# Regrouped weight loads, a first elementwise step by halves, and the last eviction and store on ScalarE, in a dense layer with GELU and its gradients

## The chip, the cores and the metric

The kernel runs on one core of a Trainium2 chip. The metric is the device time of one execution in microseconds. Five engines of the core take part: TensorE (PE in the profile, its weight loads PEld), VectorE (DVE), ScalarE (ACT), GpSimd (POOL) and SyncE (SP), which here only issues DMA transfers. Each engine works through its own instructions in the order in which the program issued them. An instruction that has to wait for another engine or for a transfer holds up all that stands behind it on its own engine.

## The reference

A dense layer with a tanh-approximated GELU is computed, and then the gradients of its five inputs for a given `grad_out`:

```python
B, S, D, F = 1, 2048, 448, 1792        # all bf16
h   = gelu(x @ w1 + b1)                # [S, F]
out = h @ w2 + b2                      # out_0 [S, D]
# gradients of x, w1, b1, w2, b2 for grad_out g [S, D]:
gh  = (g @ w2.T) * gelu'(x @ w1 + b1)  # [S, F]
gx  = gh @ w1.T                        # out_1
gw1 = x.T @ gh ; gb1 = sum(gh, rows)   # out_2, out_3
gw2 = h.T @ g  ; gb2 = sum(g, rows)    # out_4, out_5
```

## The kernel before

The 2048 rows are cut into four blocks b of 512. In each block the 1792 columns of the hidden layer are cut into 14 tiles of 128, taken two at a time, so that a block has seven steps and the whole run has 28, numbered g = 0 to 27. In a step the hidden columns lie on the 128 partitions; its two tiles of 128 columns are the halves h = 0 and 1, each with the 512 rows of the block along a partition, so that an elementwise instruction over a whole step has 1024 elements per partition, and one over a half 512.

The work of one step g, with the names that the text uses:

- `M1(g)` (L213, matmuls L221) and the first half of `rest` (L224, L231) compute u = x w1 in PSUM for both halves: three matmuls of 128 deep and one of 64 each. `rest` (L234) and `M4(g)` (L237, L240) compute q = g w2^T in the same way. There is one buffer for u and one for q. Only for g = 0 does u lie in two tiles of the accumulator pool `acc` instead.
- `act_first` (L243) runs on ACT: V = u + b1 for each half (L247), A = Square of V scaled (L248), hT = GELU of V (L249).
- `dve_first` (L251) runs on DVE: B = (A + const) * V (L252), p = (A + const) * hT (L253), p - 0.5 (L254).
- `act_second` (L256) runs on ACT: t = tanh of B (L257). `dve_second` and `dve_third` (L260, L263) then make t + 1 and the product with p.
- `dve_gate(g)` (L266), called the gate in the text, multiplies with q from PSUM and writes ghT(g).
- `run_pieces` runs the second matmuls (`Unit.piece`, L297). A unit gathers 128 rows of `out` over all 14 tiles of hT, or 128 rows of `gx` over all 14 tiles of ghT, one piece for one tile. In block 0 the four units of `out` grow along with the steps, two pieces each in a step, eight in all; these are called pieces(g). They need hT(g) and rows of w2: pieces(0) need row tiles 0 and 1 of w2, pieces(1) tiles 2 and 3, and so on.

V, A, B have one buffer for all steps, t and p two. The tiles are slices of large flat tensors.

The loop at L359 writes the order out by hand. For step g it issues, on their engines: `rest(g+1, g)`, `M4(g)`, the gate of g, the first ACT and DVE parts of g+1, tanh and the products of g+1, pieces(g), and `M1(g+2)`. At g = 7, `M1(9)` comes ahead of the pieces. Step 0 has no step ahead of it: `M1(0)`, `rest(0)` and its whole elementwise chain stand before the loop (L351 to L358).

All loads of block 0 but those of L168 to L170 are issued on SP in one order (L167, L172 to L175, L186 to L200). Some are plain (`load_w1`: two transfers each, `load_w2`: one), others transposing (`load_x`, `load_g`, `load_w2T`: two each, `load_w1T`: one). `load_w1(f0, f1)` and `load_w2T(f0, f1)` bring the columns f0 to f1 of the hidden layer, of which step g of block 0 uses 256, from 256 g on; `load_w2(t0, t1)` brings row tiles t0 to t1 of w2.

After the 28 steps follow the remaining units, then gw1 (L452, L460), then gw2: 14 tiles of 16 matmuls each (L471), evicted by ACT (L473) and stored by SP. The last of the 14 is evicted by ACT and DVE, half each (L480, L481), and stored by SP (L482).

Of the kernel before, what the change touches and what calls it, by code (L numbers as in the profile page):

```python
# [8 lines left out]
ACT = mybir.ActivationFunctionType  # L9
ALU = mybir.AluOpType  # L10
# [3 lines left out]
GELU_A = 0.044715  # L14
GELU_C = math.sqrt(2.0 / math.pi)
# [3 lines left out]
def kernel(  # L19
# [15 lines left out]
    nc = tc.nc  # L35
    P = 128
    B, S, D = x.shape
# [3 lines left out]
    NF = F // P  # L41
# [8 lines left out]
    NPAIR = NF // 2  # L50
# [8 lines left out]
    out4_v = out_4.rearrange("(ft p) d -> p ft d", p=P)  # L59
# [26 lines left out]
    b1_col = const.tile([P, NF], F32, name="b1_col")  # L86
# [8 lines left out]
    gw2_all = w2_sb  # L95
# [11 lines left out]
    def ring(t, n, g):  # L107
        o = (g % n) * 2 * SB
        return t[:, o:o + 2 * SB].rearrange("p (h s) -> p h s", h=2)

    def hT(g):
        return ring(hT_flat, HR, g)
# [4 lines left out]
    def V_of(g):  # L117
        return VA_flat[:, 0:2 * SB].rearrange("p (h s) -> p h s", h=2)

    def A_of(g):  # L120
        return VA_flat[:, 2 * SB:4 * SB].rearrange("p (h s) -> p h s", h=2)

    def B_of(g):
        return ring(B_flat, 1, g)

    def t_of(g):
        return ring(T_flat, 4, 2 * (g % 2))

    def p_of(g):
        return ring(T_flat, 4, 2 * (g % 2) + 1)  # L130
# [11 lines left out]
    def load_g(b):  # L142
        rows = slice(b * SB, (b + 1) * SB)
        nc.sync.dma_start_transpose(out=gq(b)[:, KF, :], in_=g2[rows, DOV:D])
        nc.sync.dma_start_transpose(out=gq(b)[:, 0:KF, :], in_=g2[rows, 0:DM])  # L145

    def load_w1(eng, f0, f1):
        eng.dma_start(out=w1_sb[:, 0:KF, f0:f1], in_=w1[DL:D, f0:f1].rearrange("(k p) f -> p k f", p=P))
        eng.dma_start(out=w1_sb[0:DL, KF, f0:f1], in_=w1[0:DL, f0:f1])

    def load_w2(eng, t0, t1):
        eng.dma_start(out=w2_sb[:, t0:t1, :], in_=w2[t0 * P:t1 * P, :].rearrange("(t p) d -> p t d", p=P))

    def load_w2T(f0, f1):
        nc.sync.dma_start_transpose(out=w2T_sb[:, KF, f0:f1], in_=w2[f0:f1, DOV:D])  # L155
        nc.sync.dma_start_transpose(out=w2T_sb[:, 0:KF, f0:f1], in_=w2[f0:f1, 0:DM])  # L156
# [14 lines left out]
    nc.scalar.activation(out=T_flat[0:1, SB + 2:SB + 3], in_=ones, func=ACT.Gelu_apprx_tanh)  # L171
    load_g(0)  # L172
    load_w2T(0, 256)
    load_w1(nc.sync, 512, 768)
    load_w2(nc.sync, 0, 2)  # L175
    pw = psum_a.tile([P, SB], F32, name="acc")
    for i in range(8):
        nc.tensor.matmul(pw[:], lhsT=warm[:, 0:P], rhs=warm, start=True, stop=True)
# [4 lines left out]
    nc.vector.tensor_copy(out=b1_col[:], in_=pb[:, 0:NF])  # L183
    for i in range(3):
        nc.tensor.matmul(pw[:], lhsT=warm[:, 0:P], rhs=warm, start=True, stop=True)
    load_w2T(256, 768)  # L186
    load_w2(nc.sync, 2, 6)
    load_w1(nc.sync, 768, 1280)
    load_w2T(768, 1280)
    load_w2(nc.sync, 6, 10)  # L190
    load_w1(nc.sync, 1280, F)
    load_w2T(1280, F)
    load_w2(nc.sync, 10, NF)
    nc.sync.dma_start(out=b2_bc[:], in_=b2.rearrange("(o d) -> o d", o=1).to_broadcast((P, D)))
    load_x(1)
    load_w1T(0, 4)
# [13 lines left out]
    u_of = {}  # L210
# [13 lines left out]
    def rest(gu, gg):  # L224

        if gg is not None:
            q = psum_g.tile([P, 2, SB], F32, name="q")
            g_of[gg] = q
        for h in range(2):
            if gu is not None:  # L230
                nc.tensor.matmul(u_of[gu][h], lhsT=w1_sb[0:DL, KF, cols(gu, h)], rhs=xq(gu // NPAIR)[0:DL, KF, :],  # L231
                                 start=False, stop=True, tile_position=(0, 0), skip_group_check=True)
            if gg is not None:
                nc.tensor.matmul(q[:, h, :], lhsT=w2T_sb[DL:P, KF, cols(gg, h)], rhs=gq(gg // NPAIR)[DL:P, KF, :],  # L234
                                 start=True, stop=False, tile_position=(DL, 0), skip_group_check=True)
# [7 lines left out]
    def act_first(g):  # L243
        u = u_of.pop(g)
        for h in range(2):
            ft = 2 * (g % NPAIR) + h
            nc.scalar.activation(out=V_of(g)[:, h, :], in_=u[h], func=ACT.Identity, bias=b1_col[:, ft:ft + 1])  # L247
        nc.scalar.activation(out=A_of(g), in_=V_of(g), func=ACT.Square, scale=math.sqrt(3.0 * GELU_C * GELU_A))  # L248
        nc.scalar.activation(out=hT(g), in_=V_of(g), func=ACT.Gelu_apprx_tanh)  # L249

    def dve_first(g):  # L251
        nc.vector.scalar_tensor_tensor(out=B_of(g), in0=A_of(g), scalar=3.0 * GELU_C, in1=V_of(g), op0=ALU.add, op1=ALU.mult)  # L252
        nc.vector.scalar_tensor_tensor(out=p_of(g), in0=A_of(g), scalar=GELU_C, in1=hT(g), op0=ALU.add, op1=ALU.mult)  # L253
        nc.vector.tensor_scalar(out=p_of(g), in0=p_of(g), scalar1=-0.5, scalar2=None, op0=ALU.add)  # L254

    def act_second(g):  # L256
        nc.scalar.activation(out=t_of(g), in_=B_of(g), func=ACT.Tanh, scale=-1.0 / 3.0)  # L257

    def dve_second(g):
        nc.vector.tensor_scalar(out=t_of(g), in0=t_of(g), scalar1=1.0, scalar2=None, op0=ALU.add)  # L260
# [89 lines left out]

    M1(0)  # L351
    rest(0, None)
    act_first(0)
    dve_first(0)
    act_second(0)
    dve_second(0)
    dve_third(0)
    M1(1)  # L358
    for g in range(NSTEP):  # L359
# [10 lines left out]
        if nxt is not None:  # L370
            act_first(nxt)
# [71 lines left out]
    for t0, t1 in ((0, 4), (4, HT)):  # L443
        n = (t1 - t0) * P
        for h in range(2):
            a0, a1 = t0 + h * HT, t1 + h * HT
            cs = slice(a0 * P, a1 * P)
            for kt in range(KF):
                ps = psum_a.tile([P, SB], F32, name="acc")
# [6 lines left out]
        ps = psum_a.tile([P, SB], F32, name="acc")  # L456
# [6 lines left out]
        for h in range(2):  # L463
            nc.scalar.dma_start(out=out_2[KF * P:D, (t0 + h * HT) * P:(t1 + h * HT) * P],
                                in_=gw1_rem[h * DL:(h + 1) * DL, t0 * P:t1 * P])


    for ft in range(NF):
        ps = psum_a.tile([P, SB], F32, name="acc")
        for st in range(NS):  # L470
            nc.tensor.matmul(ps[:, 0:D], lhsT=h_blk[ft][:, st, :], rhs=g_all[:, st, :], start=(st == 0), stop=(st == NS - 1))  # L471
        if ft < NF - 1:
            nc.scalar.copy(out=gw2_all[:, ft, :], in_=ps[:, 0:D])  # L473
            if ft % 3 == 2:
                nc.sync.dma_start(out=out4_v[:, ft - 2:ft + 1, :], in_=gw2_all[:, ft - 2:ft + 1, :])
            if ft == NF - 2:
                nc.sync.dma_start(out=out4_v[:, ft:ft + 1, :], in_=gw2_all[:, ft:ft + 1, :])
        else:
            hd = D // 2
            nc.scalar.copy(out=gw2_all[:, ft, 0:hd], in_=ps[:, 0:hd])  # L480
            nc.vector.tensor_copy(out=gw2_all[:, ft, hd:D], in_=ps[:, hd:D])  # L481
            nc.sync.dma_start(out=out4_v[:, ft, :], in_=gw2_all[:, ft, :])  # L482


# [28 lines left out]
```

## Time and profile before

| | |
|---|---|
| median of 3 runs | 278.21 us (277.89 to 278.37) |
| profiled execution, its own time | 278.12 us |
| span of the profile | 276.3 us |
| PE busy in the span | 266.2 us, 96% |
| DVE, ACT, POOL busy | 188.6, 144.5, 50.9 us |
| DVE busy from 7.7 to 14.1 us | 3.83 of 6.40 us |
| DVE busy from 14.1 to 49.8 us | 34.29 of 35.70 us |
| PE busy from 49.8 to 272.7 us | 222.23 of 222.90 us |
| mean granted clock of TensorE | 1.00 |

The page gives the whole span, from the first to the last instruction; the time of an execution has some 1.8 us around it. Instructions that issue transfers are not counted as busy; the profile shows them with a q behind the engine's name (SPq, ACTq). A transfer's landing is counted from the start of its issue. The loads on SP that the change touches, in the order of their issue, as the trace has them:

| load | issued at (us) | issue took (us) | landed after (us) |
|---|---|---|---|
| w2T 0:256, two transposes | 6.66, 7.94 | 1.24, 1.28 | 2.8, 2.9 |
| w1 512:768, two | 9.27, 9.91 | 0.58, 0.56 | 2.8, 2.9 |
| w2 tiles 0:2 | 10.51 | 0.58 | 3.0 |
| w2T 256:768, two | 11.13, 12.34 | 1.16, 1.49 | 3.5, 4.1 |
| w2 tiles 2:6 | 13.87 | 0.58 | 5.78 |
| w1 768:1280, two | 14.51, 15.05 | 0.50, 0.49 | 6.2, 5.9 |
| w2T 768:1280, two | 15.59, 16.90 | 1.27, 3.74 | 5.9, 5.9 |
| w2 tiles 6:10 | 20.69 | 0.59 | 6.0 |
| w1 1280:1792, two | 21.33, 21.87 | 0.50, 0.51 | 6.5, 6.3 |
| w2T 1280:1792, two | 22.42, 25.39 | 2.92, 2.33 | not shown, 4.3 |
| w2 tiles 10:14 | 27.77 | 0.59 | 4.0 |
| b2 | 28.40 | 0.49 | 4.0 |
| x of block 1, two | 28.94, 31.27 | 2.29, 1.26 | 5.1, 3.8 |

### The profile page before, as it was taken

What the parts mean: (1) busy time and instruction counts of PE and PEld (TensorE: products, weight loads), DVE (VectorE), ACT (ScalarE), POOL (GpSimd) and SP (SyncE); (2) the same over time, 40 slices, a digit from 0 to 9 for tenths busy, and PEclk for the clock granted to TensorE, in tenths of its full rate; (3) what the DMA queues carried; (4) which work ended last, traced back from release to release, by engine and by line L of the source; (5) the groups of instructions that cost most, each with busy time, mean ns of one, the idle gap of its engine ahead of it and who ended that gap; (6) DMA issues with size and microseconds to landing.
All of it is one profiled execution on the core that took longest, in us unless ns stands there. A gap on an engine that the chain in (4) does not pass through costs nothing.

```text
span 276.3 us, 3567 instructions
## 1 busy us (share of the span) xinstructions
PE 266.2 (96%) x1389; PEld 123.4 (45%) x1403; DVE 188.6 (68%) x217; ACT 144.5 (52%) x188; POOL 50.9 (18%) x54
## 2 busy tenths in 40 slices
PE   8689999999999999999999999999999999999994
PEld 3234443344344444444444445554444655555552
DVE  0599999999989999999887881109999990000000
ACT  2887888788888878887677750021102121111111
POOL 0000000840120403032030234111510009600000
PEclk9999999999999999999999999999999999999999
DMA  8799999999789955335634329999999971101110
GB/s 168 175 210 209 225 209 186 212 340 154 150 219 188 260 76 120 65 123 118 168 112 78 109 79 214 229 365 208 171 238 250 237 176 57 51 1 50 50 52 33
DMA packets 101571, 43.78 MB, mean 158 GB/s; under 512 B 90161, under 2 KB 98161, under 8 KB 101554
## 3 DMA queue, kind: packets, MB, share of 16 engines
q1 hardware_dynamic: 94224, 26.80, 52.9%
q0 software_dynamic: 4448, 14.69, 17.2%
q10 hardware_dynamic: 2882, 2.07, 2.7%
q8 instruction: 11, 0.18, 0.3%
q14 instruction: 6, 0.05, 0.0%
HBM read 7.00 MB, written 14.23 MB: 77 GB/s over the span
## 4 chain that ended last, share of the span: by engine, by line
PE 82%; DVE 6%; SPq 5%; DMA 2%; ACT 2%; issue 2%; DVEq 0%
PE acc L297 27%; PE acc L471 15%; PE acc L452 13%; PE q L240 11%; PE u L221 9%; PE u L231 4%; PE acc L460 2%; DMA w_gw<-in_w_dram 2%; DVE ghT_h L266 2%; DVE Bt L252 2%; DVE T L253 1%; SPq L156 1%; SPq L155 1%; DVE T L263 1%; SPq L145 1%
## 5 line engine op out<-in xcount | busy, mean ns | idle before, releaser
L297 PE MATMUL acc<-w_gw,hT_h 128*128 128x448 bf16 x224 | 46.1, 352 | 2.4 <-ACT VA L247 1.3
L297 PE MATMUL acc<-w1T_gw,ghT_h 128*128 128x448 bf16 x224 | 45.2, 352 | 0.0
L247 ACT ACTIVATE VA<-u,b_col 128x512 f32<-128x512 f32 x54 | 34.1, 681 | 15.5 <-PE u L231 14.8
L240 PE MATMUL q<-xg_h,w2T_g 128*128 128x512 bf16 x167 | 40.9, 381 | 1.0 <-DMA w2T_g<-in_w_dram 0.8
L266 DVE SCALAR_TENSOR_TENSOR ghT_h<-T,q 128x1024 bf16<-128x1024 bf16 x28 | 34.2, 1220 | 8.8 <-PE q L240 7.6
L221 PE MATMUL u<-xg_h,w_x 128*128 128x512 bf16 x149 | 38.4, 379 | 1.2 <-ACT VA L247 0.6
L252 DVE SCALAR_TENSOR_TENSOR Bt<-VA 128x1024 f32<-128x1024 f32 x28 | 34.1, 1219 | 5.0 <-ACT VA L248 5.0
L452 PE MATMUL acc<-gh_nat,w_x 128*128 128x512 bf16 (+1 forms) x192 | 36.7, 353 | 0.0
L257 ACT ACTIVATE T<-Bt 128x1024 bf16<-128x1024 f32 x28 | 29.6, 1057 | 12.8 <-DVE Bt L252 12.7
L253 DVE SCALAR_TENSOR_TENSOR T<-VA,hT_h 128x1024 bf16<-128x1024 f32 x28 | 34.1, 1219 | 0.0
L297 PEld LDWEIGHTS <-hT_h 128*128 128x128 bf16 x224 | 21.8, 98 | 24.4 <-ACT VA L247 1.8
L297 PEld LDWEIGHTS <-ghT_h 128*128 128x128 bf16 x224 | 21.9, 98 | 20.8
L481 DVE CAST w_gw<-acc 128x224 bf16<-128x224 f32 x1 | 0.4, 391 | 44.5 <-ACT w_gw L480 44.5
L437 DVE TENSOR_TENSOR VA<-VA,gh_nat 128x1792 f32<-128x1792 f32 x14 | 30.0, 2142 | 0.5
L248 ACT ACTIVATE VA<-VA 128x1024 f32<-128x1024 f32 x28 | 29.6, 1057 | 0.9
L249 ACT ACTIVATE hT_h<-VA 128x1024 bf16<-128x1024 f32 x28 | 29.1, 1040 | 0.0
L452 PEld LDWEIGHTS <-w_x 128*128 128x128 bf16 x192 | 18.7, 98 | 17.8 <-issue 0.4
L240 PEld LDWEIGHTS <-w2T_g 128*128 128x128 bf16 x168 | 14.1, 97 | 26.0 <-issue 11.5
L221 PEld LDWEIGHTS <-w_x 128*128 128x128 bf16 x168 | 16.3, 98 | 19.5 <-issue 1.5
L473 ACT CAST w_gw<-acc 128x448 bf16<-128x448 f32 x13 | 6.9, 533 | 32.6 <-PE acc L471 32.6
L317 POOL DMA_DIRECT2D out_dram<-io_o x8 | 6.0, 748 | 95.7 <-DVE io_o L313 48.3
L454 ACT CAST w1T_gw<-acc 128x512 bf16<-128x512 f32 (+1 forms) x12 | 6.2, 533 | 30.2 <-PE acc L452 17.1
(52 smaller groups left out, 245.8 us busy)
## 6 DMA issues: line engine op xcount, KB each, us to landing
hT_dram<-hT_h POOLq DMA_DIRECT2D x28, 256.0 KB, 4.0
out_dram<-io_o POOLq DMA_DIRECT2D x8, 224.0 KB, 4.7
out_dram<-io_g POOLq DMA_DIRECT2D x8, 224.0 KB, 2.9
w_x<-in_x_dram POOLq DMA_DIRECT2D x1, 1792.0 KB, 12.8
w2T_g<-in_grad_out_dram POOLq DMA_DIRECT2D x1, 1792.0 KB, 16.7
w_gw<-in_w_dram SPq DMA_DIRECT2D x3, 448.0 KB, 5.0
out_dram<-w_gw SPq DMA_DIRECT2D x4, 336.0 KB, 2.4
w_x<-in_w_dram SPq DMA_DIRECT2D x2, 384.0 KB, 6.4
```

The lines of the kernel that those rows point to most:

```text
L221: nc.tensor.matmul(u_of[g][h], lhsT=w1_sb[:, kt, cols(g, h)], rhs=xq(g // NPAIR)[:, kt, :], start=(kt == 0), stop=False, skip_group_check= ...
L240: nc.tensor.matmul(g_of[g][:, h, :], lhsT=w2T_sb[:, kt, cols(g, h)], rhs=gq(g // NPAIR)[:, kt, :], start=False, stop=(kt == KF - 1), skip_ ...
L247: nc.scalar.activation(out=V_of(g)[:, h, :], in_=u[h], func=ACT.Identity, bias=b1_col[:, ft:ft + 1])
L248: nc.scalar.activation(out=A_of(g), in_=V_of(g), func=ACT.Square, scale=math.sqrt(3.0 * GELU_C * GELU_A))
L252: nc.vector.scalar_tensor_tensor(out=B_of(g), in0=A_of(g), scalar=3.0 * GELU_C, in1=V_of(g), op0=ALU.add, op1=ALU.mult)
L253: nc.vector.scalar_tensor_tensor(out=p_of(g), in0=A_of(g), scalar=GELU_C, in1=hT(g), op0=ALU.add, op1=ALU.mult)
L257: nc.scalar.activation(out=t_of(g), in_=B_of(g), func=ACT.Tanh, scale=-1.0 / 3.0)
L266: nc.vector.scalar_tensor_tensor(out=ghT(g), in0=t_of(g), scalar=1.0, in1=g_of.pop(g)[:], op0=ALU.add, op1=ALU.mult)
L297: nc.tensor.matmul(self.ps[:, 0:D], lhsT=lhsT, rhs=rhs, start=(ft == 0), stop=(ft == NF - 1 and not bias))
L437: nc.vector.tensor_tensor(out=gsb_v, in0=gsb_v, in1=gh_rows(st, 0, NF), op=ALU.add)
L452: nc.tensor.matmul(psv, lhsT=x_all[:, st, kt * P:(kt + 1) * P], rhs=gh_rows(st, a0, a1), start=(st == 0), stop=(st == NS - 1))
L471: nc.tensor.matmul(ps[:, 0:D], lhsT=h_blk[ft][:, st, :], rhs=g_all[:, st, :], start=(st == 0), stop=(st == NS - 1))
```

## The change

Three things are changed. On SP, tiles 0 and 1 of w2 are loaded ahead of w1's columns 512 to 768; w2T's columns 256 to 768 come in two loads instead of one, the second of them behind w1's columns 768 to 1280; and the other loads of w2 bring tiles 2:4, 4:8 and 8:14 instead of 2:6, 6:10 and 10:14. The elementwise chain of step 0 is issued by halves, in a new function that takes the place of `act_first(0)`, `dve_first(0)` and `act_second(0)`. The last tile of gw2 is evicted whole by ACT, and stored by a transfer issued on ACT.

```diff
     load_w2T(0, 256)
+    load_w2(nc.sync, 0, 2)
     load_w1(nc.sync, 512, 768)
-    load_w2(nc.sync, 0, 2)
...
-    load_w2T(256, 768)
-    load_w2(nc.sync, 2, 6)
+    load_w2T(256, 512)
+    load_w2(nc.sync, 2, 4)
     load_w1(nc.sync, 768, 1280)
+    load_w2T(512, 768)
+    load_w2(nc.sync, 4, 8)
     load_w2T(768, 1280)
-    load_w2(nc.sync, 6, 10)
     load_w1(nc.sync, 1280, F)
     load_w2T(1280, F)
-    load_w2(nc.sync, 10, NF)
+    load_w2(nc.sync, 8, NF)
     nc.sync.dma_start(out=b2_bc[:], in_=b2.rearrange("(o d) -> o d", o=1).to_broadcast((P, D)))
...
+    def first_by_halves(g):
+        u = u_of.pop(g)
+
+        def V(h):
+            ft = 2 * (g % NPAIR) + h
+            nc.scalar.activation(out=V_of(g)[:, h, :], in_=u[h], func=ACT.Identity, bias=b1_col[:, ft:ft + 1])
+
+        def A(h):
+            nc.scalar.activation(out=A_of(g)[:, h, :], in_=V_of(g)[:, h, :], func=ACT.Square,
+                                 scale=math.sqrt(3.0 * GELU_C * GELU_A))
+
+        def H(h):
+            nc.scalar.activation(out=hT(g)[:, h, :], in_=V_of(g)[:, h, :], func=ACT.Gelu_apprx_tanh)
+
+        V(0)
+        A(0)
+        V(1)
+        H(0)
+        A(1)
+        H(1)
+        for h in (0, 1):
+            nc.vector.scalar_tensor_tensor(out=B_of(g)[:, h, :], in0=A_of(g)[:, h, :], scalar=3.0 * GELU_C,
+                                           in1=V_of(g)[:, h, :], op0=ALU.add, op1=ALU.mult)
+            nc.scalar.activation(out=t_of(g)[:, h, :], in_=B_of(g)[:, h, :], func=ACT.Tanh, scale=-1.0 / 3.0)
+            nc.vector.scalar_tensor_tensor(out=p_of(g)[:, h, :], in0=A_of(g)[:, h, :], scalar=GELU_C,
+                                           in1=hT(g)[:, h, :], op0=ALU.add, op1=ALU.mult)
+        nc.vector.tensor_scalar(out=p_of(g), in0=p_of(g), scalar1=-0.5, scalar2=None, op0=ALU.add)
...
     M1(0)
     rest(0, None)
-    act_first(0)
-    dve_first(0)
-    act_second(0)
+    first_by_halves(0)
     dve_second(0)
     dve_third(0)
...
         else:
-            hd = D // 2
-            nc.scalar.copy(out=gw2_all[:, ft, 0:hd], in_=ps[:, 0:hd])
-            nc.vector.tensor_copy(out=gw2_all[:, ft, hd:D], in_=ps[:, hd:D])
-            nc.sync.dma_start(out=out4_v[:, ft, :], in_=gw2_all[:, ft, :])
+            nc.scalar.copy(out=gw2_all[:, ft, :], in_=ps[:, 0:D])
+            nc.scalar.dma_start(out=out4_v[:, ft, :], in_=gw2_all[:, ft, :])
```

## The prediction

> **What bounds the kernel now.** I read the page first, then PE's waits, the chain in order of time, the timelines of the first step, and the landings of the loads.
>
> The page, and the waits of PE in its first 50 us (columns: who waited, for whom, us in total, times, longest):
>
> ```profile
> span 276.3 us, 3567 instructions
> PE 266.2 (96%) x1389; PEld 123.4 (45%) x1403; DVE 188.6 (68%) x217; ACT 144.5 (52%) x188; POOL 50.9 (18%) x54
> ```
> ```profile
> PE acc L297 <- ACT VA L247: 1.3, 1, 1.3
> PE acc L297 <- DMA w_gw<-in_w_dram: 1.1, 1, 1.1
> PE q L240 <- DMA w2T_g<-in_w_dram: 0.8, 1, 0.8
> PE u L221 <- ACT VA L247: 0.6, 1, 0.6
> ```
>
> Asked from 50 us on, PE has only one wait, 0.2 us. So the last entry above, M1(9) at 49.77, is the gate of the run: from there PE works through to 272.67, and what counts is when V(8) lets it start. The chain in order of time shows what sets that (start, us, what):
>
> ```profile
> 13.87 5.78 DMA w_gw<-in_w_dram
> 19.69 1.67 PE acc L297 x8
> 23.20 1.42 PE q L240 x6
> 24.64 1.22 DVE ghT_h L266
> 25.86 1.14 DVE Bt L252
> ...
> 29.75 1.22 DVE ghT_h L266
> ...
> 34.88 1.22 DVE ghT_h L266
> ...
> 40.00 1.22 DVE ghT_h L266
> ...
> 48.47 0.19 ACT VA L247
> ...
> 49.77 1.46 PE u L221 x6
> ```
>
> The gates (L266) come every 5.12 us: DVE is full (busy 34.29 of the 35.70 us from 14.1 to 49.8) and paces block 0. The exception is gate(2) at 24.64, 5.43 after gate(1) at 19.21: DVE waited for q, and q was late because PE had waited until 19.69 for w2's row tiles 2 to 5. Ahead of that stands the first step, where DVE is not full (3.83 of 6.40 us from 7.7 to 14.1):
>
> ```profile
> 7.71 1.27 ACT L247 ACTIVATE VA<-acc,b_col 128x512 f32<-128x512 f32 x2 [2.61 <-PE acc L231]
> 9.01 1.06 ACT L248 ACTIVATE VA<-VA 128x1024 f32<-128x1024 f32 x1
> 9.97 1.04 ACT L249 ACTIVATE hT_h<-VA 128x1024 bf16<-128x1024 f32 x1
> ```
> ```profile
> 10.10 1.23 DVE L252 SCALAR_TENSOR_TENSOR Bt<-VA 128x1024 f32<-128x1024 f32 x1 [5.02 <-ACT VA L248]
> 11.24 1.22 DVE L253 SCALAR_TENSOR_TENSOR T<-VA,hT_h 128x1024 bf16<-128x1024 f32 x1
> 14.09 1.22 DVE L266 SCALAR_TENSOR_TENSOR ghT_h<-T,q 128x1024 bf16<-128x1024 bf16 x1
> ```
>
> B sits idle until the whole square is ready. So the run is: V(0) at 7.71, set by x's landing (untouched); the first chain to gate(0); six DVE periods plus one stall; then PE. A gain in block 0 counts fully only if it shortens the first chain or the stall.
>
> **Part 1, the first step by halves.** Three whole ACT instructions become four halves (V was already two), tanh two, B and p two each; the -0.5, +1, product and gate stay whole. Half durations: PSUM copies on ACT take 587 ns at 512 columns and 480 at 384, 0.84 per column, so the square at 1057 ns for 1024 gives 1057 - 512 x 0.84 = 0.63 us. DVE: 391 ns at 224, 619 at 448, 1.02 per column; 1219 for 1024 gives 0.69. Independent neighbours overlap 0.10 on ACT (L249 begins at 9.97, L248 ends at 10.07) and 0.08 on DVE; a dependent one follows 0.03 after. ACT: V0 7.71 to 8.39, A0 8.42 to 9.05, V1 8.95 to 9.63, H0 9.53 to 10.16, A1 10.06 to 10.69, H1 10.59 to 11.22. DVE: B0 9.08 to 9.77; p0 waits for H0, 10.19 to 10.88; B1, queued behind that wait, 10.80 to 11.49; p1 11.41 to 12.10. Before, p ended at 12.46: gain 0.36. Tanh's halves follow H1 and B1 (11.65 to 12.28), in time for +1 at 12.48. V(1) on ACT starts near 12.2 (12.32 before), and A(1) ends at 14.5, ahead of the new end of gate(0), 14.95; q(0) is ready at 12.35. Bounds: had every half no overlap (six ACT halves of 0.68, H1 at 11.8, p1 at 12.5), gain 0; the most is 0.5, since A(1) caps B(1) at about 14.6 against 15.23 and p1 cannot end before H1 plus 0.69. I take 0.36.
>
> Here the Trainium skill (Perfetto Trace Analysis, Optimizing Scalar/DVE Operations) speaks both ways: it wants operations grouped where an engine is saturated and broken up where it is not but makes others wait; the first step is the second kind, later steps the first. The page ScalarE: Activation LUTs (What ACT_TABLE_LOAD costs) has 186 ns plus 0.833 per element, an estimated 613 ns for a half, which would make the gain about 0.4.
>
> **Part 2, the loads on SP.** One load of w2T (256 to 768) becomes two, that is two more transposes of 1.16 to 1.28 us of SP time when nothing pushes back: 2.44 in all. w2's four loads stay four, regrouped 2, 2, 4, 6 row tiles instead of 2, 4, 4, 4. New order on SP: w2[0:2] at 9.27, landing 3.0 later (as its row) at 12.3; M4(0) ends at 12.35, so PE's wait of 1.29 before 13.64 goes (the profile blames V; the landing 10.51 + 3.0 = 13.5 is the real releaser). w1 for M1(2) goes behind it: 0.62 later, landed by 13.4, wanted at 14.07. w2T[256:512]: issued 11.13 and 12.3, landing 3.5 and at most 4.1 later, 16.4; M4(1) wants it near 16. w2[2:4]: issued 13.65. Its row waited 3.25 beyond w2T's landing (16.4 to 19.65) with twice the bytes behind twice the transposes; halved, it lands near 17, wanted at 17.5 to 18. w1[768:1280] had landed at 20.95; two quarter-megabyte pieces fewer are ahead of it. From 13.5 to 31.8 the queue landed 3.66 MB, 200 GB/s, so 2.3 us less: 18.7, wanted at 19.2. w2T[512:768]: issued 15.3 and 16.5, between 19.5 and 22.4 (the 5.9 of its row). M4(2) must start by 22.4, so gate(2) no longer waits: gain 5.43 - 5.12 = 0.31. If w2[2:4] still took 5.78 it would land at 19.45, and only 0.2 of the sum of both parts would be left.
>
> What is late next? The total of bytes is the same, and the DMA engines are full (share 1.15 of the window 14.1 to 49.8). SP's transposes at 16.90, 22.42 and 25.39 took 3.74, 2.92 and 2.33, together 5.2 above a free one, pushed back by a full queue; the added 2.44 is taken from that. Without push-back the last w2 load would be issued at 24.5 (27.77 before). Its tiles 8 and 9, formerly landed at 26.7, now come with it at 31.8 to 32.3; pieces(4) want them at 33.2, and PE can wait until 34.4 before gate(5) does (from pieces at 33.93 to q's end at 38.84 are 4.91; gate(5) is due at 39.33). x(1), landed at 35.1 and wanted at 39.5, and w1T follow with margins of 4 us and more.
>
> Against this part the Trainium skill (DMA: Bandwidth & Descriptors, Rules for kernel authors) says to coalesce, since under 64 KB a transfer is mostly overhead. The split pieces are 64 and 192 KB, and rows of those sizes landed in 2.8 and 2.9, so a fixed part dominates here too. By the rows the sum below stands, as the fixed part is SP's time; by the rule, were it taken out of the full queue, the slower rival (c) would be the outcome.
>
> **Part 3, the tail.** Now ACT's half (272.69, 0.35) and DVE's (273.07, 0.39) run one after the other, and SP issues at 273.49. A whole copy takes 0.533 (L473): ACT issues at 273.25, 0.24 earlier. SP's store of 112 KB lands after 1.7; ACT's own of 48 KB after 1.9, issue 0.47 to 0.61 against 0.345. Gain 0.04 to 0.24; I take 0.14, the middle. Nothing is queued behind it on ACT but the final drain.
>
> **Sum.** 0.36 + 0.31 + 0.14 = 0.81, off the profiled execution's 278.12 (span 276.3 and 1.8 around it): 277.3. The median is 278.21, so 277.4. Bounds of the terms: 0.35 to 1.05.
>
> **Rivals.** (a) Halves gain nothing, since the fixed part of each eats the overlap: 0.45, 277.8. For it: ACT is already 5.98 of 6.40 busy there. (b) w2[2:4] is as late as ever behind the transposes: 0.2 + 0.14, 277.9. Against it: less is in flight. (c) Slower: w2[8:14] lands too late. If SP's 2.44 is not absorbed, it is issued at 30.2 and lands after 4.0 to 6.0, at 34.2 to 36.2. Past 34.4 gate(5) waits, past 35.2 the whole gain is gone; at 36.2 it is 279.2, at 35.9 278.9. Against it: the 5.2 us of push-back. (d) The halves are ordered like wholes: if B0 waits for A1 (10.72) and p0, B1, p1 follow in 0.61 steps, p ends at 13.24, 0.78 later than before; 278.5. For it: the last eviction's two halves did run one after the other (they share a PSUM bank); against it: L257 and L253 write T side by side at 11.36.
>
> **How the numbers follow.** My case 0.62, (a) 0.15, (b) 0.08, (c) 0.09, (d) 0.06. The runs before spread 277.89 to 278.37, so 0.2% (0.56 us, the least a measurement tells from no change) is a boundary at 277.65. My case alone is 277.0 to 277.8 with the spread, and lies under the boundary some nine times in ten; with a third of (a) and a quarter of (b), faster is 0.64. The rest of those and half of (d) are the same, 0.25; most of (c) and the rest of (d), slower, 0.11. The range runs from 276.9 (1.05 and the spread) to 278.3, past (a) and (b), leaving (c) and (d) out.
>
> **What would show it.** gate(0) near 13.7 instead of 14.09; no PE wait before the first pieces and pieces(1) near 17.5; gate(2) 5.12 after gate(1); M1(9) at 49.1; then PE without a wait, 222.9 us to its last matmul; ACT's last copy one row of 0.53. Wrong, if gate(5) or an earlier gate waits for q after a late landing, if B0 starts after A1, or if M1(9) comes earlier and PE stalls later, in block 1, where SP's transposes stand behind the loads.

## The result, and the profile after

The changed kernel takes 277.68 us at the median of 11 runs (276.88 to 277.95), the kernel before 278.19 (277.84 to 278.49, 11 runs). The ratio is 0.9977, 95% interval 0.9969 to 0.9984: 0.64 us less, between 0.45 and 0.86. (The ratio is not simply that of the two medians, which differ by 0.51.) So there is a gain, of about the 0.56 us that the prediction took as the least a measurement tells from no change. The forecast was 277.4, range 276.9 to 278.3.

The profiled execution of the changed kernel took 277.43 us, against 278.12. Its page:

```profile
span 275.7 us, 3572 instructions
PE 266.6 (97%) x1389; PEld 123.4 (45%) x1403; DVE 188.4 (68%) x218; ACT 144.7 (52%) x191; POOL 50.9 (18%) x54
```

The timeline of DVE and ACT in the first step (start us, us, engine, line, operation, output and input, count):

```profile
8.10 0.69 ACT L257 ACTIVATE VA<-acc,b_col 128x512 f32<-128x512 f32 x1 [3.01 <-PE acc L232]
8.81 0.63 ACT L260 ACTIVATE VA<-VA 128x512 f32<-128x512 f32 x1
9.48 0.69 DVE L273 SCALAR_TENSOR_TENSOR Bt<-VA 128x512 f32<-128x512 f32 x1 [4.05 <-ACT VA L260]
10.57 0.69 DVE L276 SCALAR_TENSOR_TENSOR T<-VA,hT_h 128x512 bf16<-128x512 f32 x1 [0.40 <-ACT hT_h L264]
11.18 0.69 DVE L273 SCALAR_TENSOR_TENSOR Bt<-VA 128x512 f32<-128x512 f32 x1
11.78 0.68 DVE L276 SCALAR_TENSOR_TENSOR T<-VA,hT_h 128x512 bf16<-128x512 f32 x1
14.09 1.22 DVE L295 SCALAR_TENSOR_TENSOR ghT_h<-T,q 128x1024 bf16<-128x1024 bf16 x1
```

DVE begins 1.38 us after V instead of 2.39, and gate(0) comes 5.99 after V(0) instead of 6.38. But V(0) itself began at 8.10 instead of 7.71, so gate(0) has the same 14.09 as before. The code ahead of V(0) is the same in both kernels; the 0.39 is a chance of this execution, as the experiments show.

The gates of the changed kernel, from DVE's timeline, and PE's waits in its first 55 us:

```profile
19.21 1.22 DVE L295 SCALAR_TENSOR_TENSOR ghT_h<-T,q 128x1024 bf16<-128x1024 bf16 x1
24.33 1.22 DVE L295 SCALAR_TENSOR_TENSOR ghT_h<-T,q 128x1024 bf16<-128x1024 bf16 x1
```
```profile
PE acc L326 <- DMA w_gw<-in_w_dram: 1.6, 1, 1.6
PE q L241 <- DMA w2T_g<-in_w_dram: 1.0, 1, 1.0
PE u L222 <- ACT VA L248: 0.5, 1, 0.5
```

From gate(0) to gate(6) at 44.81 the gates stand 5.12 apart, the one of 24.33 included: DVE no longer waits for q. PE's two waits for w2, 1.3 and 1.1 before, are gone, and a new one of 1.56 has come up at 24.04, for tiles 4 to 7 (pieces(2)). It delays no gate: q(3) is still ready 0.5 before gate(3), and DVE sets the pace. M1(9) begins at 49.46 instead of 49.77, and from there PE needs 222.90 us to its last matmul in both profiles. Then the tail, from the timelines before and after:

```profile
272.69 0.35 ACT L480 CAST w_gw<-acc 128x224 bf16<-128x224 f32 x1 [2.49 <-PE acc L471]
273.07 0.39 DVE L481 CAST w_gw<-acc 128x224 bf16<-128x224 f32 x1 [44.54 <-ACT w_gw L480]
273.49 0.34 SPq L482 DMA_DIRECT2D out_dram<-w_gw  x1
```
```profile
272.38 0.53 ACT L506 CAST w_gw<-acc 128x448 bf16<-128x448 f32 x1 [2.49 <-PE acc L498]
272.94 0.36 ACTq L507 DMA_DIRECT2D out_dram<-w_gw  x1
```

The store is issued 0.58 after PE's end at 272.36, where it was 0.82 (273.49 after 272.67), and lands 1.7 later, as SP's did. From PE's end to the end of the span are 3.30 us instead of 3.68 (the traces have the spans as 275.66 and 276.35). The difference of the two spans is thus +0.39 (V(0)) - 0.39 (first step) - 0.31 (stall of gate(2)) - 0.38 (tail) = -0.69, and the times of the two executions differ by as much. The earlier issue explains 0.24 of the tail's 0.38; the run with the tail alone shows where the rest comes from.

### The profile page after: what moved, and what is told of

The parts are those of the page before. It is cut to its first block, busy times and chain, and to the rows that moved or that the text cites. A ratio compares the mean times of both kernels' runs of the same rounds, so it can differ in the third digit from the quotient of the medians.

```text
span 275.7 us, 3572 instructions
## 1 busy us (share of the span) xinstructions
PE 266.6 (97%) x1389; PEld 123.4 (45%) x1403; DVE 188.4 (68%) x218; ACT 144.7 (52%) x191; POOL 50.9 (18%) x54
## 4 chain that ended last, share of the span: by engine, by line
PE 88%; SPq 6%; DMA 2%; issue 1%; DVE 1%; ACT 1%
PE acc L326 30%; PE acc L498 15%; PE acc L479 13%; PE q L241 12%; PE u L222 11%; PE u L232 4%; PE acc L487 2%; DMA w_gw<-in_w_dram 2%; SPq L156 1%; SPq L155 1%; SPq L145 1%; SPq L139 1%; SPq L144 0%; SPq L140 0%; DVE ghT_h L295 0%
## 5 line engine op out<-in xcount | busy, mean ns | idle before, releaser
L286 ACT ACTIVATE T<-Bt 128x1024 bf16<-128x1024 f32 x27 | 28.5, 1057 | 12.8 <-DVE Bt L281 12.7
L281 DVE SCALAR_TENSOR_TENSOR Bt<-VA 128x1024 f32<-128x1024 f32 x27 | 32.9, 1218 | 0.0
L282 DVE SCALAR_TENSOR_TENSOR T<-VA,hT_h 128x1024 bf16<-128x1024 f32 x27 | 32.9, 1218 | 0.0
L249 ACT ACTIVATE VA<-VA 128x1024 f32<-128x1024 f32 x27 | 28.5, 1057 | 0.9
L250 ACT ACTIVATE hT_h<-VA 128x1024 bf16<-128x1024 f32 x27 | 28.1, 1040 | 0.0
L299 POOL DMA_DIRECT2D hT_dram<-hT_h x28 | 20.6, 736 | 0.7 <-ACT hT_h L250 0.7
```

## The experiments

Every run comes with a profile, and this sum holds in each of them: span = V(0)'s start, plus V(0) to gate(0), plus six times 5.12, plus the stall, plus 4.65 from gate(6) to M1(9), plus 222.90 on PE, plus the tail. (The stall is what a gap between two gates up to gate(6) has over 5.12.) Only the run in which w2 came late on purpose breaks it, by 0.48.

| run | ratio to before (95%) | time of the profiled execution (median) | V(0) | V(0) to gate(0) | stall | tail |
|---|---|---|---|---|---|---|
| before | 1 | 278.12 (278.21) | 7.71 | 6.38 | 0.31 | 3.68 |
| changed | 0.9977 (0.9969 to 0.9984) | 277.43 (277.68) | 8.10 | 5.99 | 0 | 3.30 |
| halves alone | 0.9992 (0.9982 to 1.0001) | 278.80 (278.05) | 7.88 | 6.00 | 1.19 | 3.68 |
| loads alone | 0.9997 (0.9987 to 1.0007) | 278.41 (278.01) | 8.49 | 6.37 | 0 | 3.52 |
| tail alone | 0.9993 (0.9984 to 1.0001) | 277.60 (277.73) | 7.73 | 6.38 | 0 | 3.46 |
| w2 first alone | 1.0009 (0.9996 to 1.0022) | 277.86 (278.13) | 7.72 | 6.38 | 0.05 | 3.68 |
| w2 late | 1.0107 (1.0084 to 1.0130) | 280.97 (281.02) | 8.41 | 6.00 | 2.74 | 3.30 |
| split | 0.9964 (0.9949 to 0.9978) | 277.49 (277.40) | 8.17 | 6.00 | 0 | 3.26 |
| x freed | 0.9980 (0.9964 to 0.9997) | 277.44 (277.62) | 8.10 | 6.00 | 0 | 3.31 |
| x freed and split | 0.9976 (0.9960 to 0.9992) | 278.34 (277.44) | 7.35 | 7.70 | 0 | 3.25 |
| halves and tail | 0.9987 (0.9978 to 0.9997) | 277.56 (277.90) | 7.92 | 6.00 | 0.15 | 3.47 |
| changed again | 0.9974 (0.9962 to 0.9985) | 277.87 (277.59) | 8.56 | 5.99 | 0 | 3.30 |
| split, fewer warming matmuls | 0.9971 (0.9957 to 0.9984) | 277.18 (277.42) | 7.88 | 6.00 | 0 | 3.24 |

(The tail goes from the end of PE's last matmul to the end of the span, with the spans to 0.01 us as the traces have them. A profile shows one execution. Two of these are far from the median of their kernel: that of the halves alone is the longest of eleven, that of x freed and split is among the three longest of twelve.)

**Halves alone**

```diff
-    act_first(0)
-    dve_first(0)
-    act_second(0)
+    first_by_halves(0)
```

> Only the first step by halves; loads and tail as before. My theory: two things stand one behind the other in block 0, the first chain on DVE and the stall of gate(2) for q, which hangs on the landing of w2's row tiles 2 to 5 at 19.65, an absolute time that the halves do not move. So from V(0) to gate(0) it is 6.0 us instead of 6.38, but gate(2) waits about 0.75 instead of 0.41 and comes where it came: M1(9) and the time within 0.15 us of before. Rival, the parts add up: gate(2) also 0.36 earlier, time 0.36 us less (ratio 0.9987). Rival, halves cost: ratio over 1.001 and gate(0) later.

The first step is 0.38 shorter, and gate(2) waits 1.3 us for q (1.19 beyond the 5.12 after gate(1)):

```profile
DVE ghT_h L294 <- PE q L240: 1.3, 1, 1.3
```

Its PE timeline shows the reason in the wait before pieces(1), until w2's tiles 2 to 5 had landed:

```profile
20.37 1.67 PE L325 MATMUL acc<-w_gw,hT_h 128*128 128x448 bf16 x8 [1.50 <-DMA w_gw<-in_w_dram]
```

That is 0.68 later than in the profile before, and the stall grew by more than the halves gave. As this profile is of the longest of the eleven executions (278.80 us, the median is 278.05), a stall of 1.19 is not the usual one. The ratio, 0.9992, lies between my theory and the additive rival (0.22 us less, the interval from nothing gained to 0.5; the two medians, 278.05 and 278.04, show no gain). That the halves cost time is out; how much of the 0.38 comes through on average this run alone doesn't say.

**Loads alone**

```diff
     load_w2T(0, 256)
+    load_w2(nc.sync, 0, 2)
     load_w1(nc.sync, 512, 768)
-    load_w2(nc.sync, 0, 2)
...
-    load_w2T(256, 768)
-    load_w2(nc.sync, 2, 6)
+    load_w2T(256, 512)
+    load_w2(nc.sync, 2, 4)
     load_w1(nc.sync, 768, 1280)
+    load_w2T(512, 768)
+    load_w2(nc.sync, 4, 8)
...
-    load_w2(nc.sync, 6, 10)
...
-    load_w2(nc.sync, 10, NF)
+    load_w2(nc.sync, 8, NF)
```

> Only the loads regrouped; first step and tail as before. My theory: gate(2) no longer waits for q, 5.12 after gate(1) instead of 5.43, and M1(9) 0.31 earlier relative to V(0): ratio 0.9989. Rival, PE paces block 0: PE loses its waits of 1.29 and 1.14 and gains a wait for w2's tiles 4 to 7, so 0.9 us less or more. Rival, nothing is left of it: 1.000.

Gate(2) doesn't wait, all gates are 5.12 apart, as expected; but the time is 0.9997 of before, not 0.9989. The expected 0.31 lies just at the edge of the interval. PE pacing block 0, 0.9 us less or more, is excluded. Why the gain is smaller is seen in the next two runs: the old order doesn't have the stall in every execution. (V(0) began at 8.49 in this profile, so gate(2) was due 0.78 later than in the profile before. But pieces(1) began at 17.96 without a wait, 1.73 earlier than before, so with this landing no stall would have come up with an early V(0) either.)

**Tail alone**

```diff
-            hd = D // 2
-            nc.scalar.copy(out=gw2_all[:, ft, 0:hd], in_=ps[:, 0:hd])
-            nc.vector.tensor_copy(out=gw2_all[:, ft, hd:D], in_=ps[:, hd:D])
-            nc.sync.dma_start(out=out4_v[:, ft, :], in_=gw2_all[:, ft, :])
+            nc.scalar.copy(out=gw2_all[:, ft, :], in_=ps[:, 0:D])
+            nc.scalar.dma_start(out=out4_v[:, ft, :], in_=gw2_all[:, ft, :])
```

> Only the last eviction and store on ScalarE. My theory: from PE's last matmul to the store's issue 0.56 instead of 0.82 us, landing 1.7 after it from either queue, so 0.24 us less: ratio 0.9991, and the time from PE's end to the end of the span 3.3 instead of 3.6 us. Rival, a store from ACT lands later by what the issue saved: 1.000.

The ratio is 0.9993, 0.2 us less with an interval that just includes none. The profiles are sharper, and they fall into groups:

| tail, from PE's end (us) | old load order | regrouped loads | regrouped and split loads |
|---|---|---|---|
| old tail | 3.68 in all three | 3.52 (loads alone) | |
| new tail | 3.46, 3.47 | 3.30, 3.30, 3.30, 3.31 | 3.24, 3.25, 3.26 |

So the edit of the tail is worth 0.22, nearly the whole of the earlier issue, with the old loads and with the new ones. And the regrouped loads, which lie at the start of the run, take another 0.16 off its end, which nothing in the forecast stands for. Most of that lies between the landing of the last store and the end of the span: 1.15 to 1.17 us in the five profiles of the old order (w2 first alone is one of them), 0.98 to 1.03 in the eight others. What the engines do there, and why the load order changes it, was not followed up.

The profile of this run holds a surprise: with the old load order, gate(2) didn't wait in it at all:

```profile
19.23 1.22 DVE L266 SCALAR_TENSOR_TENSOR ghT_h<-T,q 128x1024 bf16<-128x1024 bf16 x1
24.35 1.22 DVE L266 SCALAR_TENSOR_TENSOR ghT_h<-T,q 128x1024 bf16<-128x1024 bf16 x1
```

The stall of 0.31 that the forecast took from one execution is no constant of the kernel.

**w2 first alone**

```diff
-    load_w1(nc.sync, 512, 768)
     load_w2(nc.sync, 0, 2)
+    load_w1(nc.sync, 512, 768)
```

> Only w2's tiles 0 and 1 ahead of w1's columns 512 to 768, nothing split or regrouped. My theory: PE's wait of 1.29 before the first pieces goes, but the next one, until w2's tiles 2 to 5 land at 19.65, grows by as much and gate(2) stays where it was: time within 0.15 us of before. Rival, PE paces: 1.3 us less (ratio 0.9954).

1.0009, so nothing is gained: PE's wait before the first pieces is gone, it waits 1.4 before the second ones instead, and the stall is 0.05. As PE's wait moved rather than vanish, it is the run of the loads alone, in which both waits are gone, that excludes PE as the pace of block 0.

**Halves and tail, without the loads**

The first and third of these edits together, the loads as before.

> The changed kernel without its regrouped loads: halves and tail alone. My theory after the first runs: the stall of gate(2) is nought in some executions of the old load order, but with halves gate(1) comes 0.39 earlier against a landing that does not move, so the stall takes back most of what the halves gain (1.19 us in the profile of the halves alone). Ratio 0.9982 to 0.999: the tail's 0.25 and little of the 0.39. Rival, the parts add up and the loads are worth nothing: 0.9977, and no stall in the profile.

**The changed kernel again**, on the same chip:

> The changed kernel once more, for comparison on the same chip: ratio 0.9977 as on record, gates 5.12 apart, V(0) to gate(0) 6.0 us, and V(0) somewhere between 7.7 and 8.5 by the moment at which TensorE's clock comes up. Rival, its gain was an accident of that moment: ratio over 0.999.

0.9987 without the regrouped loads, 0.9974 with them. The two intervals (0.9978 to 0.9997, 0.9962 to 0.9985) overlap at their edges, so the 0.36 us between them is likely but not certain. The rival that the loads are worth nothing (0.9977) lies just outside the first interval, and the rival that the gain was an accident (over 0.999) outside the second. Beside V(0), the two profiles differ by 0.17 in the tail (3.47 against 3.30) and by a stall of 0.15. But that stall is not at gate(2), where my theory had it:

```profile
19.19 1.22 DVE L294 SCALAR_TENSOR_TENSOR ghT_h<-T,q 128x1024 bf16<-128x1024 bf16 x1 [0.26 <-PE q L240]
24.31 1.22 DVE L294 SCALAR_TENSOR_TENSOR ghT_h<-T,q 128x1024 bf16<-128x1024 bf16 x1
```

It is gate(1) that came 0.15 late, as PE had stood 1.4 us, until 14.24, for w2's tiles 0 and 1. Gate(2) followed 5.12 later, and pieces(1) began at 18.99 without waiting for a load. So the landing of tiles 2 to 5 is no fixed time: of the five profiles with those tiles in one load, pieces(1) began at 18.68 and 18.99 without waiting for it (tail alone, halves and tail), and at the end of a wait at 19.45, 19.69 and 20.37 (w2 first alone, before, halves alone). In these last three gate(2) came 4.94 or 4.95 after pieces(1). With the regrouped loads pieces(1) waited for no load in any of the eight profiles, and gate(2) did not stall.

From this it can be worked out, though no run shows it by itself, that with the same landing a chain shorter by 0.39 makes the stall of gate(2) longer by as much, once there is one. Whether the parts of the change add up in the usual execution stays open: by the ratios the three edits alone give 0.22, 0.08 and 0.20, together 0.50, against 0.64 and 0.72 for the whole, and each interval is some 0.5 wide.

**w2 late**, the price of the slower rival:

```diff
     load_w2T(1280, F)
-    load_w2(nc.sync, 8, NF)
...
     load_x(1)
+    load_w2(nc.sync, 8, NF)
```

> The changed kernel with w2's last load (row tiles 8 to 13) moved behind the transposes of block 1's x: the price of the slower rival (c). My theory: in the changed kernel pieces(4) began at 33.73, just behind the landing at 33.7, and q(5) was ready 1.05 before gate(5). So every us of the landing past 34.8 is paid in full: issued near 33, landed at 37 to 39, it makes gate(5) late by 2.2 to 4.2 and the run as much longer (ratio to the kernel before 1.006 to 1.013). Rival, PE catches up on the way to M1(9): ratio below 1.000.

1.0107, 3.0 us more than before, in the range that my theory gave; the rival that PE catches up is excluded. But the working was off. The load was issued earlier than I had thought, 31.23, and landed at 36.1, which by the slack should have cost 36.1 - 34.8 = 1.3, or 1.1 with the later V(0) of this execution counted in. Gate(5) came 2.74 late and the span gained another 0.48 behind it. The rest is TensorE's clock. From PE's timeline, and the busy time by stretches (span of the stretch, its length, busy us and instructions of PE, PEld, DVE, ACT and POOL, granted clock, share and rate of the DMA engines):

```profile
36.16 1.90 PE L326 MATMUL acc<-w_gw,hT_h 128*128 128x448 bf16 x8 [3.02 <-DMA w_gw<-in_w_dram]
37.86 2.77 PE L222 MATMUL u<-xg_h,w_x 128*128 128x512 bf16 x6
```
```profile
34.00:38.00 4.00, 1.83 (x9) 0.97 (x9) 3.86 (x5) 3.10 (x4) 0.00 (x0) 0.93 1.09 263
38.00:41.50 3.50, 3.50 (x13) 0.90 (x12) 1.83 (x4) 0.43 (x2) 0.00 (x0) 0.59 1.07 163
41.50:45.00 3.50, 3.50 (x19) 1.71 (x18) 2.25 (x2) 3.17 (x4) 0.00 (x0) 1.00 1.22 212
```

After a wait of 3.0 us the granted clock fell. The 0.59 is a mean over the stretch: the trace's record of the clock has 0.50 from 37.48 to 40.89, and full clock before and behind. Six matmuls of M1 took 2.77 instead of 1.46, and from the start of pieces(4) to the end of q(5) were 6.55 us instead of 4.91. That is 1.64 more, and with the 1.1 it makes the 2.74. The 0.48 is PE's as well: from 36.16 to M1(9) at 53.01 the profile has no wait on PE, so it was PE that set the pace there.

**Split**

```diff
-    load_w2T(512, 768)
-    load_w2(nc.sync, 4, 8)
+    load_w2(nc.sync, 4, 6)
+    load_w2T(512, 768)
+    load_w2(nc.sync, 6, 8)
```

> The changed kernel with w2's tiles 4 and 5 loaded ahead of w2T's columns 512 to 768, and 6 and 7 behind them: PE's wait of 1.56 until 24.04, which the change brought in, should shrink below 0.5. My theory, DVE paces block 0 and q(3) was ready 0.5 before gate(3) anyhow: the time stays that of the changed kernel (ratio to before 0.997 to 0.9985, the gates 5.12 apart). Rival, PE's wait is what the change paid for its gain: ratio below 0.995.

PE's wait for tiles 4 to 7 is gone: pieces(2) began at 22.48 without one. (The 0.7 that PE still waits for w2 is for tiles 8 to 13, before pieces(4).) The gates stayed 5.12 apart, and from V(0) to M1(9) are 41.37 us, against 41.36 in the changed kernel. The ratio, 0.9964, is the best of all, but its interval (0.9949 to 0.9978) takes in that of the changed kernel; no cause for a gain can be seen in its profile but a tail shorter by 0.04. PE's wait is not what the change paid with, as without it M1(9) came no earlier after V(0).

**x freed**

```diff
-    load_w1(nc.scalar, 256, 512)
     nc.scalar.activation(out=T_flat[0:1, SB + 2:SB + 3], in_=ones, func=ACT.Gelu_apprx_tanh)
+    load_w1(nc.scalar, 256, 512)
```

> The changed kernel with w1's columns 256 to 512 issued on ScalarE behind the warming activation instead of ahead of it, so that less is in flight beside x's transposes. My theory: the run hangs on V(0), which began between 7.71 and 8.49 in the six profiles so far with the same code ahead of it, since x's second transpose landed at different times; with less beside it V(0) begins at 6.8 to 7.4, gate(0) follows 6.0 later, and each us is gained until q or a load is late: 0.3 to 1.2 us less than the changed kernel, unless gate(3) waits for q, as w2's tiles 4 to 7 still land near 24 (then about 0.5 less). Rival, x's landing is set by its own issue on SP: V(0) as before, ratio to the kernel before 0.9977 again.

**x freed and split**

> The last two together. My theory: with the earlier V(0) PE's wait for w2's tiles 4 to 7 does count, so together they gain 0.3 to 0.5 us more than the earlier w1-free start alone; ratio to the kernel before 0.993 to 0.9965. Rival, the loads after it are as late as ever and gate(2) or gate(3) waits for another of them: no more than the run before this.

Neither gains over the changed kernel (0.9980 and 0.9976). The first part of the theory held: x's second transpose landed 3.9 to 4.0 us after its issue, near 6.1, in both profiles, instead of the 5.1 to 5.6 of all the others, so the rival's reason, that x's landing is set by its own issue, is excluded. But something else was late each time. In the first, V(0) began at 8.10: PE was late, with its warming matmuls at 1.28 us instead of 0.82, as the last section shows. In the second, V(0) began at 7.35, the earliest of all, but M1(1) waited 2.5 us for w1's columns 256 to 512 (2.0 in the first), the clock fell again (0.59 in the mean from 10 to 14 us), q(0) was late, and gate(0) came 7.70 after V(0), at 15.05. From DVE's waits:

```profile
DVE ghT_h L296 <- PE q L242: 1.8, 1, 1.8
```

This profile is of one of the three longest executions of twelve (278.34 us; nine lie from 276.89 to 277.63), so it shows how the early start can be lost, not what the median execution does.

**Split, with fewer warming matmuls**

```diff
-    for i in range(3):
-        nc.tensor.matmul(pw[:], lhsT=warm[:, 0:P], rhs=warm, start=True, stop=True)
     load_w2T(256, 512)
```

> The changed kernel with w2's tiles 4 to 7 in two loads as in the run before it, and without the three warming matmuls between the bias and M1(0). My theory: in the profiles with a late V(0) (8.4 to 8.5) TensorE was still at half its clock until about 7.4 and these three took 1.46 us instead of 0.82 just ahead of M1(0); without them M1(0) starts as x lands, V(0) is at 7.3 to 7.9 whatever the moment of the clock, and the slow executions vanish: 0.1 to 0.4 us less at the median than the split alone, ratio 0.9945 to 0.9965. Rival, with less work ahead of it the clock comes up later: V(0) at 8.0 or later, ratio 0.9975 or over.

0.9971: not told apart from the split or the changed kernel. V(0) was at 7.88, within the expected 7.3 to 7.9, set by x's landing. But the spread did not vanish: of its twelve times seven lie from 277.05 to 277.44 and five from 278.07 to 278.43. The one profile is of the first group, so what the five have in common stays open.

## Why the prediction was right, and where it was off

**The first chain** (0.36): right, 0.39 and 0.38 in the profiles. DVE's halves fell as worked out, counted from V(0): B0 1.38 after it (worked out 1.37), p1's end 4.36 (4.39). ACT's halves took 0.62 to 0.63 from SBUF (worked out 0.63). The order on ACT, and p0's wait of 0.40 for H0 with B1 queued behind it, are there.

**The stall of gate(2)** (0.31): the mechanism was right, as gate(2) comes 4.94 or 4.95 after pieces(1) in each of the three profiles in which it stalls, and the regrouped loads take the stall away. The size was read from one execution and taken for the kernel's: three profiles of the old order of w2's tiles 2 to 5 without halves have 0.31, 0 and 0.05. And the sum added it to the first chain, as if the chain had no part in it; with the halves and the old order it was 1.19, in the longest of eleven executions, and 0 (with 0.15 at gate(1)). How large it is in the usual execution, with the halves or without, stays open.

**The tail** (0.14, bounds 0.04 to 0.24): mis-sized, 0.22 by the tail alone. ACT's store landed 1.7 after its issue, like SP's, not 1.9, and its issue took 0.36, not 0.47 to 0.61; the rows taken for it were of other shapes, with other stores beside them. So nearly the whole 0.24 of the earlier issue came through.

**The loads' part of the tail** was not in the sum: 0.16, between 3.68 and 3.52 with the old tail and between 3.46 and 3.30 with the new.

**The loads, what is late next.** w2[8:14] was foreseen at 31.8 to 32.3 and landed at 33.7, just before pieces(4) began at 33.73. For w2[4:8] the working gives no landing, though tiles 4 and 5, which came with 2 and 3 before, now come with 6 and 7: they landed at 23.99, and PE's wait of 1.56 is theirs. Until 18.3 SP issued as worked out, only 0.2 to 0.4 later and with no push-back; then its transposes at 20.11, 26.18 and 29.10 took 3.54, 1.66 and 3.87. The queue was full again, and emptied later than the sum of bytes at 200 GB/s had it. DVE's pace covered it, with 0.5 us of q's slack left at gate(3) and 1.05 at gate(5). Rival (c) did not come, but the run with w2 late shows that it would have cost more than its price of one us for each us past the slack. (a), (b) and (d) are excluded, by the first step's 5.99, by pieces(1) at 17.48 and by B0 at 9.48, ahead of A1 at 10.44.

**Gate(0) near 13.7, M1(9) at 49.1**: seen at 14.09 and 49.46, since V(0)'s start was taken as fixed at 7.71. It is not.

**The sum**: 0.81 forecast, 0.64 and 0.72 measured (0.9977 and 0.9974). The first chain's 0.39, the tail's 0.22 and the loads' 0.16 at the end make 0.77 with a stall of nought. So a stall that was too large by up to 0.3, a tail too small by 0.08 and 0.16 from a place that the sum did not look at nearly cancelled. That the forecast came this close is in part luck.

## What to carry to other kernels

A wait for a transfer has the size of one execution: before its price enters a sum, see it in a second profile, and ask whether the other parts of the change move its ends, for then the terms need not add. See too where the time of the profiled execution lies among the others of its kernel. Where engines run through fixed stretches one behind the other, write the span as their sum (here first data, first chain, DVE's periods, PE's stretch, tail); it then tells in one line where each tenth of a microsecond of two profiles went, and shows a part of the change that acts where no term of the forecast stands, as the loads did at the end of the run. A late transfer is free as long as the pacing engine's input is ready, and past that it can cost more than its lateness.

## What the runs showed of the hardware that had not been expected

The first 8 us differ from one execution to the next, with identical instructions. V(0) began between 7.71 and 8.56 in the profiles whose code is the same up to there. One cause is x's second transpose, landing 5.1 to 5.6 us after its issue in these profiles. The other is the moment at which TensorE speeds up. PE's timeline in the profile before:

```profile
1.18 3.26 PE L178 MATMUL acc<-T 128*128 128x512 bf16 x8 [1.18 <-DVE T L165]
4.80 0.82 PE L185 MATMUL acc<-T 128*128 128x512 bf16 x3
5.46 1.46 PE L221 MATMUL acc<-xg_h,w_x 128*128 128x512 bf16 x6
```

and in the second profile of the changed kernel:

```profile
1.19 3.59 PE L178 MATMUL acc<-T 128*128 128x512 bf16 x8 [1.19 <-DVE T L165]
5.17 1.46 PE L185 MATMUL acc<-T 128*128 128x512 bf16 x3
6.42 1.78 PE L222 MATMUL acc<-xg_h,w_x 128*128 128x512 bf16 x6
```

Matmuls of 512 columns pass every 0.4 us at first and every 0.2 later. In the one execution the warming matmuls behind the bias are already fast, in the other they and the first two of M1(0) are still slow, and V(0) starts at 8.56 instead of 7.71, past x's landing. The trace's record of the granted clock begins where the pace changes: with full clock at 3.97 us in the one and at 7.07 in the other. In the thirteen profiles it does so between 3.90 and 7.07, though PE's first matmul starts at 1.18 or 1.19 in all of them. Of the twelve with the three warming matmuls in place, three show these at 1.46 us (full clock from 6.75 to 7.07), one at 1.28 (6.14), one at 1.10 (5.77) and seven at 0.82 (4.77 at the latest). In the two profiles where PE later stood still for 2.5 and 3.0 us, the clock went to 0.50 for 3.41 us, from 10.73 and from 37.48 on, that is 0.7 and 1.3 us after PE had work again. A wait of 2.0 us (x freed) was not followed by it.

The Trainium skill (TensorE: Matmul & The Clock Gate, Part 1: The HAM clock gate) describes both: the array gets half its clock until it was busy through a window of some 3.4 us that runs freely, whatever moment the kernel starts at, and again after an idle window. The traces agree with the pace, with the length of the window (3.41 us at half clock, twice) and with the spread between executions (3.17 us); here even waits shorter than a whole such window (2.5 us) were followed by the lower clock. That the phase of the window, and not something else in the start, makes each execution's difference is the page's account; no run here sets the phase.
